# The backward segment of a recurrent-memory attention block: output projection as column passes, and the segment's heads in two halves

## The chip, the cores and the metric

The kernel runs on one core of a Trainium2 chip. The metric is the device time of one execution in microseconds (us). Before the change three timed runs gave 3111.13, 3111.70 and 3111.64 us, median 3111.64. The profile shown here comes from an execution of its own that took 3105.46 us; its span, from the first to the last instruction in the trace, is 3103.7 us.

## The reference

One transformer block, forward and backward, in bfloat16 data with batch 1, 2048 tokens of 448 features, 16 heads of 256 features each, and a gated feed-forward net of 1792. Attention is recurrent: the tokens come in 64 segments of 32, and each segment attends over 8 memory rows and its own 32 rows (40 rows, `L`). The first 8 output rows of a segment are the memory of the next.

```python
for s in range(n_seg):
    h = concatenate([mem, x[:, 32*s : 32*s + 32]], axis=1)        # 8 + 32 rows
    q, k, v = (einsum('btd,dhe->bhte', h, W) for W in (Wq, Wk, Wv))
    scores = where(mask, einsum('bhqe,bhke->bhqk', q, k) * scale, -1e9)
    p = softmax(scores)
    o = einsum('bhte,hed->btd', einsum('bhqk,bhke->bhqe', p, v), Wo)
    mem, out = o[:, :8], o[:, 8:]
# h = x + attention(layernorm(x));  result = h + ffn(layernorm(h))
```

The kernel returns the block's output and the gradients with respect to `x`, `mem0`, the four attention weights and the three feed-forward weights, for a given gradient of the output.

In the backward direction the segments run from 63 down to 0, one after another, since the gradient of a segment's 8 memory rows is what the segment before it starts from. Per segment: the gradient of the output rows goes back through `Wo` (call the result dO, 40 rows of 4096 columns); dP = dO v^T and dv = p^T dO; dS = p * (dP - rowsum(dP * p)); dk and dq from dS and its transpose; and the three of them go back through `Wv`, `Wk`, `Wq` to the 40 input rows, of which the first 8 are the gradient carried to the next segment in the order.

## The kernel before

The program runs through a forward chain, the feed-forward net, the backward chain of 64 segments and a tail for the weight gradients. The change is in `backward_chain`, with one small edit in the feed-forward phase (two pad columns). Four segments make a tile of 128 tokens. `r` counts a tile's segments and goes 3, 2, 1, 0. A chunk is 128 of the 4096 head columns, so there are 32 chunks (`MC`), two per head, and the 448 features lie in 4 chunks (`KC`) of which the last holds 64.

In one segment the engines do this:

- The input is one window of `do_roll`: the transposed gradient of the 32 token rows, loaded for a whole tile by `prep_tile`, and of 8 memory rows which the segment before has written at L1226. That write is the carried gradient.
- Output projection, L1151: 128 matmuls, each with 128x128 of the transposed `Wo` as stationary side and 40 columns of `do_roll` moving. They give dO turned (`doT`), in 4 PSUM banks that DVE and ACT take out in turn. 16 transposes (L1160) make the token-major copy `dO_sb`, which ACT takes out (L1161).
- Gradients of the probabilities, L1169: 32 matmuls of `doT` with `vT` into one bank `pD`. DVE then makes the gradients of the scores in four instructions over all 8 pairs of heads, L1176 to L1181, the last of which writes the block-diagonal `dS_bd`.
- Heads, L1128 (`heads`, `head_mm`): v from `dO_sb` and the probabilities `P_bd`, k from `Q_sb` and `dS_bd`, q from `K_sb` and `dST_bd`; 16 matmuls of 80 columns each, in three banks. Each bank is taken out in two pieces, the 32 token rows into `blk` and the 8 memory rows into `lo`. Evacuations carry L75 on DVE and L76 on ACT, since one helper (`k.evac`) makes them all.
- Turned scores, L1209: 16 small matmuls with the identity turn `dS_bd` into `dST_bd`, by way of bank `pT`, a DVE and an ACT evacuation.
- Rows, L1200 (`rows_in`): 32 matmuls each for v, k and q, which run four at a time in tiles of 32 columns and all accumulate in one bank `pH`. DVE and ACT take it out (L1218, L1219), four matmuls with a selection matrix (L1222) fold the four strips, and L1226 writes the next segment's carried gradient.

Once a tile, at `r == 0`, the memory rows of the tile go through the same weights (L1264, 96 matmuls), and after L1271 and L1279 the layer norm's backward step writes 128 rows of the result (`ln_bwd`, lines L252 to L263 on DVE and ACT). These instructions have no hurry and are spread by the scheduler as fills into the following segments.

The order of instructions on every engine is fixed when the program is built. A scheduler takes the code above as a graph; what stands under `k.prio.crit()` goes first, and `tc.issue_after` ties an instruction to another. Each engine then works through its own list in order and stops where a semaphore is missing. PSUM banks come from small rings (`k.ps1`, `k.fx1`, `k.po1`), so a group of matmuls also waits until its bank's last reader is done.

Loads are issued from two queues. SP loads `vT`, `Q_sb` and `K_sb` (`load_v`, `load_seg`) for the next segment. POOL loads the segment's probabilities (`P_sb`, L1082), spreads them into `P_bd` with two copies (L1084) and issues the stores of finished tiles.

Of the kernel before, what the change touches and what calls it, by code (L numbers as in the profile page):

```python
# [9 lines left out]
FP32 = mybir.dt.float32  # L10
BF16 = mybir.dt.bfloat16
# [225 lines left out]
def cj(j):  # L237
    return (j % 2) * 16 + j // 2
# [574 lines left out]
def ffn_phase(k: _K, back):  # L813
# [32 lines left out]
    for i in range(2):  # L846
        nc.gpsimd.memset(dhb_b[i][:, D:DP], 0.0)
# [88 lines left out]
    for n, gi in enumerate(turns):  # L936
# [67 lines left out]
        for tt in range(G):  # L1004
# [16 lines left out]
            nc.scalar.copy(out=dh_b[:, 0:D], in_=dh_t)  # L1021
            nc.gpsimd.dma_start(out=dr["DHb"][rows, :], in_=dh_b)
# [9 lines left out]
def backward_chain(k: _K):  # L1032
# [9 lines left out]
    WoT_sb = W(0, KC, HD)  # L1042
# [7 lines left out]
    dO_sb = A(52, 16, P)  # L1050
    doT = A(56, 32, 64)
# [5 lines left out]
    P_bd, dS_bd, dST_bd = [B(1.25 * i, 8, 2, L) for i in range(3)]  # L1057
    Pb = [B(3.75 + 0.625 * i, 8, L) for i in range(2)]

    def prep_tile(t):  # L1060
        if t < 0:
            return
        nc.sync.dma_start_transpose(out=dhx, in_=dr["DHb"][t * P:(t + 1) * P, :])
        s0 = (4 * t) % NWIN
        for kc in range(KC):
            nc.gpsimd.tensor_copy(out=do_roll[:, kc, s0:s0 + 4, 0:SEG], in_=dhx[:, kc, :].rearrange("p (g j) -> p g j", g=4))

# [3 lines left out]
    def load_seg(s):  # L1071
# [8 lines left out]
        P_sb = Pb[s % 2]  # L1080
        with tc.issue_after(k.pool_op.ins) if s == NSEG - 1 else nullcontext():
            nc.gpsimd.dma_start(out=P_sb.rearrange("p h n -> p (h n)"), in_=dr["P_all"][s])  # L1082
        for g in range(2):
            pool_op = nc.gpsimd.tensor_copy(out=P_bd[64 * g:64 * g + L, :, g, :], in_=P_sb[64 * g:64 * g + L, :, :])  # L1084
        stores("mid", s, pool_op.ins)
# [6 lines left out]
    def stores(place, seg, ins):  # L1092

        for fn in pending.pop((place, seg), []):
            with tc.issue_after(ins):
                fn()

    for tl in (Q_sb, K_sb, P_bd, dS_bd):
        nc.gpsimd.memset(tl, 0.0)
# [6 lines left out]
    nc.sync.dma_start(out=WoT_sb[:, 0:3, :], in_=dr["To"][:, 0:3, :])  # L1106
    nc.sync.dma_start(out=WoT_sb[0:64, 3, :], in_=dr["To"][0:64, 3, :])
    nc.gpsimd.memset(WoT_sb[64:P, 3, :], 0.0)
# [5 lines left out]
    nc.vector.memset(doT[:, :, L:64], 0.0)  # L1114
    nc.gpsimd.memset(dST_bd, 0.0)
    nc.gpsimd.memset(dxT[:, KC - 1, :], 0.0)
    om = k.f32("f1", DP, "omb")
    nc.gpsimd.memset(om[:], 0.0)

    def c12(ps, b):  # L1120
        n = min(12, 32 - 12 * b)
        return 12 * b, n, ps[:, 0:n * L].rearrange("p (c n) -> p c n", n=L)

    def head_mm(ps, lhs, rhs_bd, turned):
        for cl in range(16):
            b, i = divmod(cl, 6)
            at = 8 * (cl // 4 % 2) + 4 * (cl // 8) + cl % 4 if turned else cl
            nc.tensor.matmul(ps[b][:, i * 2 * L:(i + 1) * 2 * L], lhsT=lhs[:, at, :],  # L1128
                             rhs=rhs_bd[:, cl // 2, :, :].rearrange("p g n -> p (g n)"), start=True, stop=True)

    for s in range(NSEG - 1, -1, -1):
# [7 lines left out]
        if r == 2:  # L1139
            prep_tile(t - 1)  # L1140
        if s < NSEG - 1:
            load_seg(s)

        with k.prio.crit():
            pss = [k.ps1() for _ in range(4)]
            for j in range(MC):
                c = cj(j)
                b, jj = divmod(j, 8)
                for kc in range(KC):
                    with tc.issue_after(k.last_dh.ins) if s == NSEG - 1 and j == 0 and kc == 0 else nullcontext():  # L1150
                        nc.tensor.matmul(pss[b][:, jj * L:(jj + 1) * L], lhsT=WoT_sb[:, kc, c * P:(c + 1) * P],  # L1151
                                         rhs=do_roll[:, kc, sl, :], start=(kc == 0), stop=(kc == KC - 1))
            for b in range(4):
                k.evac(doT[:, 8 * b:8 * b + 8, 0:L], pss[b][:, 0:8 * L].rearrange("p (c n) -> p c n", n=L), "vsvs"[b])

            def token_major(hf):
                ph = k.ps1()[:].bitcast(BF16)
                for i in range(8):
                    c0 = 2 * (8 * hf + i)
                    nc.tensor.transpose(ph[:, i * P:(i + 1) * P], doT[:, c0:c0 + 2, :].rearrange("p c n -> p (c n)"), ident[:, :])  # L1160
                nc.scalar.copy(out=dO_sb[:, 8 * hf:8 * hf + 8, :], in_=ph.rearrange("p (c n) -> p c n", n=P))  # L1161
            token_major(0)
            token_major(1)
            pD = k.ps1()
            for h in range(8):
                for g in range(2):
                    for dc in range(DC):
                        j = 2 * (2 * h + dc) + g
                        nc.tensor.matmul(pD[64 * g:64 * g + 64, h * L:(h + 1) * L], lhsT=doT[:, j, :], rhs=vT[:, 2 * h + dc, L * g:L * g + L],  # L1169
                                         start=(dc == 0), stop=(dc == DC - 1), skip_group_check=True)  # L1170
            if s == 0:
                k.tl.grads(0)
                k.tl.outs(0, 7, 0, 6)
            pD3 = pD[:, 0:8 * L].rearrange("p (h n) -> p h n", n=L)
            prod = k.f32("f2", 8 * L, "prod")[:].rearrange("p (h n) -> p h n", n=L)
            nc.vector.scalar_tensor_tensor(out=prod, in0=pD3, scalar=k.scale, in1=P_sb, op0=ALU.mult, op1=ALU.mult)  # L1176
            rsum = smal.tile([P, 8], FP32, name="rsum")
            nc.vector.tensor_reduce(out=rsum[:], in_=prod, axis=AX.X, op=ALU.add)
            nc.vector.scalar_tensor_tensor(out=prod, in0=pD3, scalar=k.scale, in1=rsum[:].unsqueeze(2).to_broadcast([P, 8, L]),
                                           op0=ALU.mult, op1=ALU.subtract)  # L1180
            nc.vector.tensor_tensor(out=dS_bd, in0=prod.unsqueeze(2).to_broadcast([P, 8, 2, L]), in1=P_bd, op=ALU.mult)  # L1181
# [3 lines left out]
            def heads(nm, lhs, rhs):  # L1185
                pps[nm] = [k.ps1() for _ in range(3)]
                head_mm(pps[nm], lhs, rhs, nm != "v")
                for b in range(3):
                    c0, n, v = c12(pps[nm][b], b)
                    k.evac(blk[nm][:, c0:c0 + n, r * SEG:(r + 1) * SEG], v[:, :, M:L], "vsv"[b])  # L1190
                for b in range(3):
                    c0, n, v = c12(pps[nm][b], b)
                    k.evac(lo[nm][:, c0:c0 + n, r * M:(r + 1) * M], v[:, :, 0:M], "svs"[b])
                if s == 0:
                    k.tl.outs(*{"v": (7, 9), "k": (9, 10), "q": (10, 11)}[nm], 0, 6)

# [6 lines left out]
            heads("v", dO_sb, P_bd)  # L1203
            rows_in("v", WvT_sb, 0, MC)
            heads("k", Q_sb, dS_bd)
            pT = k.ps1()
            for h in range(8):
                for g in range(2):
                    nc.tensor.matmul(pT[64 * g:64 * g + L, h * L:(h + 1) * L], lhsT=dS_bd[:, h, g, :],  # L1209
# [306 lines left out]
```

## Time and profile before

| what | value |
|---|---|
| median of three runs | 3111.64 us |
| span of the profiled execution | 3103.7 us |
| mean TensorE clock granted | 0.988 |
| PE busy, whole span | 2914.8 us (94%) |
| DVE busy | 1331.6 us (43%) |
| ACT busy | 1112.6 us (36%) |
| POOL busy | 674.7 us (22%) |
| first and last carried gradient (L1226) | 1382.88 and 2394.50 us |
| first matmul of the tail that needs the backward chain's stores (L1396) | 2430.74 us |

All busy times are sums over one engine's instructions; engines work side by side, so they don't add up to the span. PE is TensorE's matmuls, PEld its weight loads. DVE is VectorE, ACT ScalarE, POOL GpSimd, and SP only issues transfers. A matmul's own duration contains its way through the array; when many follow each other, it is the distance between starts that costs time. A piece "PE psf L1151 x128" in the chain of waits is a run of 128 matmuls of line 1151, and the number before it is the time that the run holds in the chain. Releasers ("<-") name what ended an engine's idle time.

From the first to the last L1226 are 1011.62 us, with 62 distances between them: 16.32 us a segment on average, so the backward chain is about a third of the program.

### The profile page before, as it was taken

How to read it: one execution, taken by the hardware profiler on the slowest of the kernel's cores; microseconds unless marked ns; L12 is line 12 of the kernel's file. 1: busy time of each engine (PE TensorE's matmuls, PEld its weight loads, DVE VectorE, ACT ScalarE, POOL GpSimd, SP SyncE). 2: the span in 40 equal slices, each digit the busy share in tenths (PEclk: the TensorE clock that was granted, in tenths of full speed). 3: DMA queues.
4: the chain of work that ended last, by engine and by line, in shares of the span. 5: the costliest groups of instructions: out<-in, count | busy, mean ns of one | idle time of the engine just before them, and what ended most of it. 6: DMA issues, size and time to landing. Idle time of an engine off the chain costs nothing.

```text
span 3103.7 us, 108341 instructions
## 1 busy us (share of the span) xinstructions
PE 2914.8 (94%) x47640; PEld 1735.5 (56%) x47650; DVE 1331.6 (43%) x3381; ACT 1112.6 (36%) x2634; POOL 674.7 (22%) x1511
## 2 busy tenths in 40 slices
PE   5899999989988999989999999999999899999998
PEld 3555555545544555666666666666666454444443
DVE  3555455455455576654444444544445101111110
ACT  2444344344444544443434344444344001111110
POOL 2222222222222222321122111221211111212111
PEclk9999999999999999999999999999999899999999
DMA  6567756756756899984455445555544999969951
GB/s 242 136 172 178 183 162 167 191 158 167 189 161 182 276 222 228 221 298 119 133 150 143 128 137 142 143 139 136 141 138 133 284 267 244 190 181 199 192 160 57
DMA packets 739084, 550.12 MB, mean 177 GB/s; under 512 B 600052, under 2 KB 634852, under 8 KB 736180
## 3 DMA queue, kind: packets, MB, share of 16 engines
q1 hardware_dynamic: 687380, 389.19, 51.5%
q0 software_dynamic: 51232, 154.00, 14.9%
q8 instruction: 374, 6.13, 0.8%
q14 instruction: 98, 0.80, 0.1%
HBM read 168.01 MB, written 234.23 MB: 130 GB/s over the span
## 4 chain that ended last, share of the span: by engine, by line
PE 72%; issue 11%; DVE 6%; DMA 5%; ACT 4%; POOL 2%; SPq 1%; ACTq 0%; POOLq 0%; DVEq 0%
PE po L1200 7%; PE psf L1151 7%; PE psf L535 6%; PE psf L652 5%; PE po L697 4%; PE psf L1375 4%; PE psf L890 4%; PE psf L1128 4%; PE psf L1396 4%; PE fx L1264 3%; PE fx L1014 3%; PE fx L464 2%; PE psf L1222 2%; DVE arA L75 2%; PE psf L549 2%
## 5 line engine op out<-in xcount | busy, mean ns | idle before, releaser
L75 DVE CAST arA<-psf 128x256 bf16<-128x256 f32 (+3 forms) x933 | 427.2, 480 | 808.6 <-PE psf L1375 275.2
L76 ACT CAST arA<-psf 128x96 bf16<-128x96 f32 (+5 forms) x915 | 352.4, 409 | 1036.6 <-PE psf L1375 261.2
L1200 PE MATMUL po<-arW,arA 128*32 128x448 bf16 x6144 | 347.3, 355 | 4.6 <-DMA arW<-Tq 3.5
L1375 PE MATMUL psf<-arW,arA 128*128 128x512 bf16 x980 | 247.1, 380 | 0.0
L1375 PEld LDWEIGHTS <-arA 128*128 128x128 bf16 x1440 | 136.0, 98 | 164.8 <-issue 13.8
L1151 PEld LDWEIGHTS <-arW 128*128 128x128 bf16 x8192 | 213.4, 96 | 25.0 <-issue 25.0
L1151 PE MATMUL psf<-arA,arW 128*128 128x40 bf16 x8192 | 217.0, 180 | 6.2 <-DVE arA L1226 5.1
L652 PE MATMUL psf<-arW,arA 128*64 128x512 bf16 x1536 | 219.0, 386 | 0.0
L1200 PEld LDWEIGHTS <-arA 128*32 128x32 bf16 x6144 | 152.0, 96 | 115.8 <-ACT arA L76 9.4
L535 PE MATMUL psf<-arW,arA 128*32 128x512 bf16 x3072 | 193.8, 385 | 12.5 <-DVE arA L738 12.5
L76 ACT CAST arB<-psf 128x64 bf16<-128x64 f32 (+3 forms) x384 | 121.8, 318 | 153.1 <-PE psf L539 109.7
L697 PE MATMUL po<-arW,arA 128*32 128x256 bf16 (+1 forms) x4096 | 144.2, 267 | 10.5 <-DVE arA L75 7.5
L890 PE MATMUL psf<-arW 128*128 128x256 bf16 (+1 forms) x1288 | 146.3, 274 | 1.3 <-DVE arA L956 0.7
L890 PEld LDWEIGHTS <-arW 128*128 128x128 bf16 (+1 forms) x1344 | 102.4, 97 | 51.4 <-issue 40.8
L1161 ACT COPY arA<-psf 128x1024 bf16<-128x1024 bf16 x128 | 123.3, 1015 | 2.2 <-PE psf L1160 0.4
L1128 PEld LDWEIGHTS <-arW 128*128 128x128 bf16 x2048 | 86.4, 99 | 61.8 <-issue 56.9
L535 PEld LDWEIGHTS <-arA 128*32 128x32 bf16 x3072 | 70.6, 97 | 90.0 <-DVE arA L738 18.1
L76 ACT COPY arA<-psf 128x512 bf16<-128x512 bf16 (+3 forms) x142 | 84.3, 594 | 99.9 <-DVE arA L75 90.3
L464 PE MATMUL fx<-arA,arW 128*128 128x64 bf16 (+1 forms) x2048 | 84.3, 196 | 32.4 <-ACT arB L76 19.2
L697 PEld LDWEIGHTS <-arA 128*32 128x32 bf16 x4096 | 95.9, 98 | 32.9 <-DVE arA L75 10.5
L1128 PE MATMUL psf<-arB,arW 128*128 128x80 bf16 x2048 | 96.8, 201 | 13.6 <-DVE arB L1181 5.2
L1436 POOL DMA_DIRECT2D out_dram<-arA x96 | 51.7, 546 | 249.7 <-DVE arA L75 246.9
(290 smaller groups left out, 4645.7 us busy)
## 6 DMA issues: line engine op xcount, KB each, us to landing
arW<-T SPq DMA_DIRECT2D x256, 128.0 KB
X_o<-arA SPq DMA_DIRECT2D x37, 512.0 KB
T<-arA SPq DMA_DIRECT2D x64, 256.0 KB
X_v<-arA POOLq DMA_DIRECT2D x32, 512.0 KB, 4.9
X_k<-arA POOLq DMA_DIRECT2D x32, 512.0 KB, 4.0
X_q<-arA POOLq DMA_DIRECT2D x32, 512.0 KB, 3.1
out_dram<-arA POOLq DMA_DIRECT2D x90, 128.0 KB, 3.5
VG<-arA SPq DMA_DIRECT2D x64, 160.0 KB
```

The costliest lines, as they stand in the source:

```text
L75: return nc.vector.tensor_copy(out=out, in_=in_)
L76: return nc.scalar.copy(out=out, in_=in_)
L464: nc.tensor.matmul(banks[w][:, i * 64:(i + 1) * 64], lhsT=lhsT, rhs=xr[lo:hi, kc, :], start=(kc == 0 and i == 0), stop=(kc == KC - 1), ski ...
L535: nc.tensor.matmul(banks[w][32 * q:32 * q + 32, :], lhsT=hT_roll[:, kc, sl, M:L], rhs=(Wq_sb, Wk_sb)[w][:, kc, col(q, b)], start=(kc == 0) ...
L652: nc.tensor.matmul(pV[b][64 * g:64 * g + 64, 0:512], lhsT=hT_flat[:, kc, sl * L:sl * L + 64], rhs=Wv_sb[:, kc, n * 512:(n + 1) * 512], sta ...
L697: nc.tensor.matmul(pO[32 * q:32 * q + 32, 0:w], lhsT=xblk[:, j, r * SEG:(r + 1) * SEG], rhs=Wo_sb[:, cj(j), 256 * dh:256 * dh + w], start= ...
L890: nc.tensor.matmul(ps[fp][:, f2 * 256:(f2 + 1) * 256], lhsT=Wt[lo:hi, kc, c * P:(c + 1) * P], rhs=xT[lo:hi, kc, :], start=(kc == 0 and f2 ...
L1128: nc.tensor.matmul(ps[b][:, i * 2 * L:(i + 1) * 2 * L], lhsT=lhs[:, at, :], rhs=rhs_bd[:, cl // 2, :, :].rearrange("p g n -> p (g n)"), st ...
L1151: nc.tensor.matmul(pss[b][:, jj * L:(jj + 1) * L], lhsT=WoT_sb[:, kc, c * P:(c + 1) * P], rhs=do_roll[:, kc, sl, :], start=(kc == 0), stop ...
L1200: nc.tensor.matmul(pH[32 * (j % 4):32 * (j % 4) + 32, 0:D], lhsT=blk[nm][:, j, r * SEG:(r + 1) * SEG], rhs=WT[:, cj(j), :], start=(nm == " ...
L1375: nc.tensor.matmul(pa[2 * kc + g][:, 0:w], lhsT=lhs_of(b)[:, kc * P:(kc + 1) * P], rhs=rhs_of(b, g), start=(b == 0), stop=(b == nblk - 1), ...
L1396: k.last_mm = nc.tensor.matmul(pa[i][:, 0:D], lhsT=lhs_of(b, i), rhs=rhs_of(b), start=(bi == 0), stop=(bi == len(nblk) - 1))
```

## The change

The output projection is turned around for 32 of a segment's 40 rows: 24 token rows and the 8 carried ones. `do_roll` becomes the stationary side, in tiles of 32 columns, and the transposed `Wo` moves with 512 columns (`wide_pass`), into two banks; dO then comes out token-major, and 8 transposes of 128x128 in two halves (`half_turned`) give `doT`. The other 8 token rows ("rest" rows, which are known ahead) are done for four segments together, once a tile (`rest_pass`, `wide_turned`), and POOL copies one segment's share into `doT`.

The v heads become `values`: 16 matmuls with token-major dO as stationary side and 160 columns of probabilities, in two parts (rest rows with `Pq_rest`, the others with `Pq_b`) that accumulate in three banks. All six pieces are taken out by ACT. The probabilities are loaded in the layout that these matmuls need by small DMAs from POOL's queue (4 a segment in `load_p`, 16 a tile in `load_p_rest`), and `rest_probs` on DVE masks the shared rest rows for one segment. `P_bd` is gone.

Gradients of probabilities, gradients of scores, k and q heads and turned scores each run in two halves of the heads, interleaved. Score gradients take five instructions per half. A half of k or q heads has a bank of its own and shares a third one.

Further: the pad columns of the feed-forward phase's `dhb_b` are filled by a copy in place of a memset; L1222's fourth matmul becomes two of 64 columns; `do_roll` is prepared one segment earlier in the tile.

```diff
@@ backward_chain, loads
+    def load_p(s):
...
+        for q in range(4):
+            g, x = divmod(q, 2)
+            src = dr["P_all"][s, 64 * g + M:64 * g + L].rearrange("i (b x h n) -> i b x h n", b=2, x=2, n=L)
+            nc.gpsimd.dma_start(out=Pq_b[s % 2][32 * q:32 * q + 32].rearrange("p (b h) q n -> p b h q n", b=2)[:, :, :, 2 * x + g, :],
+                                in_=src[:, :, x])
@@ backward_chain, helpers
+    def wide_pass(banks, out, lhs_of, after=None):
...
+        for b in range(2):
+            for kc in range(KC - 1):
+                for q in range(4):
+                    with tc.issue_after(first.ins):
+                        nc.tensor.matmul(banks[b][32 * q:32 * q + 32, :], lhsT=lhs_of(kc, 0, P), rhs=WoT_sb[:, kc, col(q, b)],
+                                         start=False, stop=(kc == KC - 2), skip_group_check=True)
+        for b in range(2):
+            k.evac(out[:, b, :], banks[b][:], "vs"[b])
+
+    def half_turned(pt, src, dst, b):
+        for i in range(4):
+            nc.tensor.transpose(pt[:, (4 * b + i) * P:(4 * b + i + 1) * P], src[:, b, i * P:(i + 1) * P], ident[:, :])
+        k.evac(dst[:, 16 * b:16 * b + 16], pt[:, 512 * b:512 * b + 512].rearrange("p (c n) -> p c n", n=32), "vs"[b])
+
+    def rest_probs(s):
+        nc.vector.tensor_tensor(out=Pq_rest, in0=Pr_b[(s // 4) % 2].unsqueeze(2).to_broadcast([P, 4, 4, L]),
+                                in1=gmask[:, s % 4, :].unsqueeze(1).unsqueeze(3).to_broadcast([P, 4, 4, L]), op=ALU.mult)
@@ backward_chain, one segment
-            pss = [k.ps1() for _ in range(4)]
-            for j in range(MC):
...
-                        nc.tensor.matmul(pss[b][:, jj * L:(jj + 1) * L], lhsT=WoT_sb[:, kc, c * P:(c + 1) * P],
-                                         rhs=do_roll[:, kc, sl, :], start=(kc == 0), stop=(kc == KC - 1))
...
-            token_major(0)
-            token_major(1)
+            wide_pass([k.ps1(), k.ps1()], dO_sb, lambda kc, lo, hi: do_roll[lo:hi, kc, sl, M:L])
...
+            pt = k.ps1()[:].bitcast(BF16)
+            half_turned(pt, dO_sb, doT[:, :, M:L], 0)
+            pv += [k.ps1() for _ in range(3)]
+            values(1)
+            half_turned(pt, dO_sb, doT[:, :, M:L], 1)
...
+            def grad_of_probs(b):
+                for h in range(4 * b, 4 * b + 4):
...
+                            nc.tensor.matmul(pD[64 * g:64 * g + 64, h * L:(h + 1) * L], lhsT=doT_flat[:, j * L:j * L + 64],
+                                             rhs=vT[:, 2 * h + dc, L * g:L * g + L],
...
+            grad_of_probs(0)
+            grad_of_scores(0)
+            values(0)
+            grad_of_probs(1)
+            grad_of_scores(1)
+            for b in (0, 2, 1):
+                of, v = v_out(b)
+                k.evac(of(blk["v"])[:, :, :, r * SEG:(r + 1) * SEG], v[:, :, :, M:L], "s")
+                k.evac(of(lo["v"])[:, :, :, r * M:(r + 1) * M], v[:, :, :, 0:M], "s")
...
-            heads("v", dO_sb, P_bd)
-            rows_in("v", WvT_sb, 0, MC)
-            heads("k", Q_sb, dS_bd)
...
-            rows_in("k", WkT_sb, 0, 20)
-            heads("q", K_sb, dST_bd)
-            rows_in("k", WkT_sb, 20, MC)
+            rows_in("v", WvT_sb, 0, 12)
+            heads("k", Q_sb, dS_bd, 0)
+            turned_scores(0)
+            rows_in("v", WvT_sb, 12, MC)
+            if r == 0 and t > 0:
+                rest_pass()
+            heads("k", Q_sb, dS_bd, 1)
+            turned_scores(1)
+            heads("q", K_sb, dST_bd, 0)
+            rows_in("k", WkT_sb, 0, 12)
+            heads("q", K_sb, dST_bd, 1)
+            rows_in("k", WkT_sb, 12, MC)
+            if r == 0 and t > 0:
+                wide_turned(dO_rest, R)
+            if s > 0:
+                rest_probs(s - 1)
             rows_in("q", WqT_sb, 0, MC)
```

## The prediction

> **What bounds the kernel now.** I read the page's slices first (PE at 9 in nearly all of them, the granted clock at full speed), then the table of windows for the stretch in which whole backward segments run, then the chain of waits of one segment, then the waits and the costliest groups of that stretch. The windows' columns are stretch, length, and busy time of PE, PEld, DVE, ACT and POOL.
>
> ```profile
> 1420.00:1900.00 480.00, 462.21 (x10907) 329.50 (x10905) 229.24 (x582) 198.89 (x516) 98.22 (x227) 1.00 0.52 140
> ```
>
> PE is busy 96% of it, DVE 48%, ACT 41%, POOL 20%, and the DMA engines 52%. Nothing but PE's stream of instructions can be the bound, and little of it is idle. One segment's chain says how that stream runs (start, length, what):
>
> ```profile
> 1905.41 3.30 PE psf L1151 x128
> 1908.71 0.97 PE psf L1160 x16
> 1909.68 0.62 PE psf L1169 x32
> ...
> 1910.32 0.46 PE psf L1128 x8
> 1910.78 0.49 PE fx L1264 x8
> 1911.27 0.42 PE psf L1128 x8
> 1911.69 1.63 PE po L1200 x32
> ...
> 1914.04 1.05 DVE arA L75 x3
> 1915.10 0.40 DVE arB L75
> ...
> 1915.57 0.43 ACT arB L76
> ...
> 1916.04 0.73 PE psf L1128 x16
> 1916.78 2.19 PE po L1200 x43
> ```
>
> From one carried gradient (L1226) to the next are 16.03 us here. PE goes through output projection (3.30), transposes (0.97), gradients of probabilities (0.62), v heads (0.46 + 0.42), v rows, k heads, and stands in the chain almost throughout. The one real stop is 1914.04 to 1916.00: the turned scores pass DVE and ACT before the q heads start. The fills L1264 and the rows L1200 (both matmuls of 448 columns, 0.051 each) cover what they can.
>
> ```profile
> L1181 DVE TENSOR_TENSOR arB<-prod,arB 128x640 bf16<-128x640 f32 x30 | 24.7, 825 | 0.0
> L1161 ACT COPY arA<-psf 128x1024 bf16<-128x1024 bf16 x60 | 57.8, 1015 | 0.7
> L75 DVE CAST arA<-psf 128x384 bf16<-128x384 f32 x89 | 49.5, 556 | 48.1 <-PE psf L1128 48.1
> L1176 DVE SCALAR_TENSOR_TENSOR prod<-psf,arB 128x320 f32<-128x320 f32 x30 | 14.8, 492 | 53.2 <-PE psf L1169 53.2
> L1082 POOL DMA_DIRECT2D arB<-P_all x30 | 16.3, 543 | 113.4 <-DVE prod L1176 105.7 <-DVE arB L1181 7.7
> ```
>
> The last four engine rows give the prices below; their idle shares say that DVE and ACT wait for PE, not PE for them. The starts of L1226 lie 17.04, 15.83, 16.05 and 16.04 us apart, 64.96 a tile.
>
> **What the skill says.** "TensorEngine Tiling (Array Packing)", Performance Considerations, proposes for a moving side of at most 32 columns to swap the operands and run four column tiles. The trace agrees: the forward chain's L535 is such a pass (24 matmuls of 512 columns, 379 ns each, overlapping), and with L539's 8 it takes 1.75 us (803.56 to 805.31), against 3.30 for L1151. The same page, Key Properties, says that a change of tile mode drains the array; the trace shows no price for it apart: bounds 0 and 0.1 us a switch, and I take 0.05. Its PSUM Bottleneck says that after such a speed-up the evacuations may bind. "PSUM — Partial Sum Buffer", PSUM bank collisions raise a hardware error, asks to guard PSUM by bank and quadrant; that is why pieces that share a bank wait for each other's reader here. No run shows a collision.
>
> **PE's work, part by part.** Removed per segment: L1151 3.30, L1160 0.97, v heads 0.88, together 5.15. Added: the wide pass 1.75; 8 transposes at 0.97/16, 0.49; values, 16 matmuls of 160 columns, for which the nearest row is the q heads' 0.73/16 = 0.046 for 80 columns: between 0.046 and 0.1, I take 0.075, so 1.20; once a tile the rest pass and its transposes, (1.75 + 0.49)/4 = 0.56. Together 4.00, and some 4 more mode switches, 0.2. The stream is shorter by 0.95 us a segment. Gradients of probabilities, k and q heads, turned scores and rows keep their counts. L1340's two half matmuls instead of one: 0.
>
> **What stands in order on it.** Followed along the order in which the changed program issues its instructions, with the durations of the rows (an evacuation of 128x512 f32 on DVE 0.556 + 128 x 1.07 ns = 0.69, the slope from the 256 and 384 rows; half of L1176, 0.49 - 160 x 1.04 = 0.33). A segment whose carried gradient is ready at 0, r = 2:
> - wide pass to 1.9; DVE's evacuation of bank 0 1.5 to 2.2. Half-turn 0 on PE 2.4 to 2.8, its evacuation on DVE to 3.3; half-turn 1 writes the same bank and waits for it: 3.35 to 3.75. The values with the rest rows fill the gap.
> - half-turn 1's evacuation on ACT to 4.4. The first half's last gradient matmul takes 64 columns of doT from a 40-column chunk and so reads the next chunk, which ACT writes: the first half isn't free before the second. It ends at 4.9 (before: 4.9, since 3.30 + 0.97 + 0.62 = 4.89). So nothing is gained yet.
> - score gradients, half 0 on DVE: 4 steps of 0.33 and two of 0.25 to 0.31, 5.0 to 6.6; half 1 must first get pD from PE, which DVE's L1179 of half 0 holds up, then 6.6 to 8.8 with a k evacuation (0.55) and a dST evacuation (0.3) in between. Both halves are 3.2 us of DVE against 2.28 before.
> - v rows run in this time and wait for ACT's six v_out evacuations (0.48 + 0.24 + 0.38 + 0.21 + 0.48 + 0.24 = 2.03). k half 0 at 6.8, turned scores 7.1, v rows to 8.8; k half 1 and turned half 1 follow dS half 1 at 9.0, q half 0 at 9.6, q half 1 at 10.9 (it waits for ACT's last dST piece), then some 45 rows to 13.8, and the 1.6 to 2.5 us of sum, L1222 and L1226 as before: 15.4.
> So r = 2 takes 15.4 against 15.83 to 16.05, and r = 3 by the same steps 15.1: of the old stop of 1.96 us a gain of 0.4 to 0.9 is left. The two others give it back:
> - r = 1: v_out and values wait for ACT, which has the tile's copies ahead of them; G of half 0 is 0.65 later (5.6), the halves end at 9.3; 17.2 against 16.04.
> - r = 0: the layer norm's L254 (0.62), L257, L259, L260 (0.68) and L263 (2 x 0.42) stand on DVE ahead of the half-turn's evacuation and of half 0; half 0 starts at 6.4. The rest pass fills PE while half 1 is on DVE, but its transposes are added: 18.6 against 17.04.
> Sum by tile: 15.1 + 15.5 + 17.2 + 18.6 = 66.4 (r = 2 unrounded 15.46). The same walk of the order before gives 66.1 where the trace has 64.96, so its error is 2% and only the difference counts: 0.3 more. Two entries were taken high: DVE can begin bank 0 before bank 1's last matmuls, 0.13 a segment or 0.5 a tile, and the values at 0.046 would save another 0.5. That is a gain of 0.2 to 0.7 a tile; I take 0.45; times 15.75 tiles 7 us.
>
> **Other edits.** P_bd's two POOL copies (0.45 each) go; POOL gets a copy (0.5) and 4 DMA issues a segment and 16 a tile, (4 + 4) x 0.545 = 4.4 us. POOL was busy 98.2/480, or 3.3 us of a segment, so 7.3 of 16: hidden, as the pieces are issued one segment or a tile ahead. Stores queued behind them on POOL have a segment of slack. Their 512 + 64 small packets a segment, at 0.31 x 480 x 16/59888 = 0.04 us a packet on the hardware queue, are 23 us over 16 engines, 9 points more than 52%: hidden. SP gets no new DMA inside a segment. DVE's rest_probs (about 0.83, L1181's shape) replaces nothing and lies between half-turn 0 and half 0; in the chain above it ends at 4.4, before DVE is needed. FFN: a pad copy on ACT of 64 columns, 0.2 x 16, ACT isn't the bound there: 0, at most 3. Start: rest pass, transposes and copies before the first segment, 6 to 7 us of latency, in place of a 6.8 us stall (DVE waits for a store there before the first L1226 at 1382.88): -4 to +3, I take 0. End: the tail's first matmul waits 13.02 us for X_o loads whatever PE does: -1 to 0.
>
> Profiled span 3103.7, run of it 3105.46; the three timed runs are 6 us longer (3111.64), and the difference is set against these: 3111.64 - 7 = 3104.6, say 3104.
>
> **Rivals.**
> (a) The waits are hidden by fills, rows and rest pass, as the old stop largely was; then the shorter stream counts: 0.95 x 63 = 60, 3052. For it: PE at 96% today, with DVE and ACT at less than half. Against: the half chain holds eight handovers in a row where there were four. With half of it realised 3080.
> (b) DVE's queue becomes the bound in the segment's middle. The mechanism: two half chains of score gradients (3.2 us) with other evacuations between them, behind in-order layer norm and rest_probs. It decides when half 0 begins later than about 5.3 us after the carried gradient, averaged over the four segments (I have 5.0, 5.0, 5.6, 6.4, mean 5.5, with stages behind it shorter by 0.3). Each 0.3 later is 0.3 x 63 = 19: 3130; 0.5, from mode switches at 0.1 too, 3143.
> (c) POOL's or the queue's many small loads come late and the values wait: 16 issues, 8.7 us, in one segment. 2 us a tile would be 32: 3144. Against: a tile of lead.
> (d) Halving does nothing since half 0 waits for half 1's evacuation; then only the shorter stream and the longer DVE chain remain: 0.95 less 0.92, no change, 3110.
>
> **How the numbers follow.** Forecast with (d) beside it, within 20 us of 3107: 0.45, of which three fifths lie under 3105.4. (a), whole or half: 0.22. (b) 0.27 and (c) 0.06. A measurement of this kernel tells 0.2%, 6.2 us, from no change. Faster by more than that: 0.22 + 0.25 = 0.47; within: 0.17; slower: 0.33 and a little of the forecast, 0.36. The range takes half of (a) and its margin, 3062, to (b)'s far end, 3142. Cases of both signs hold most of the chance; the forecast's own range is 3088 to 3120.
>
> **What would show it.** Right: the wide pass about 1.8 us; the chain through L1176's successor twice a segment; half 0 starting near 5.0 in two segments of a tile and later in the two others; starts of the carried gradient unequal, 15 to 15.5 twice and 17 or more twice. Wrong: equal segments of 15.3 (a), PE below 90% with DVE in most of the chain (b), or DMA from P_all as a releaser (c).

## The result, and the profile after

The changed kernel is slower: median 3163.25 us (four runs, 3157.21 to 3172.47) against 3111.39 (the three runs of above and one more), a ratio of 1.0173 (95% interval 1.0146 to 1.0200). Its profiled execution has a span of 3159.7 us, 56.0 more than the one before.

Three marks in the two traces say where. The first carried gradient is written at 1396.47 us instead of 1382.88 (13.6 later). From the first to the last are 1051.4 us instead of 1011.6 (39.8 more). What follows takes 711.9 instead of 709.2 (2.7 more).

The 13.6 is too small a figure for the start, since executions differ in how far the earlier phases have got. A mark that lies ahead of the changed part, the start of DVE's last step of 3584 columns in the feed-forward phase, shows it (first two lines before, last two after):

```profile
1335.27 2.02 DVE L977 TENSOR_TENSOR arA<-arA 128x3584 bf16<-128x3584 bf16 x1
1382.88 0.19 DVE L1226 CAST arA<-psf 128x32 bf16<-128x32 f32 x1 [2.01 <-PE psf L1222]
1328.55 2.02 DVE L975 TENSOR_TENSOR arA<-arA 128x3584 bf16<-128x3584 bf16 x1
1396.47 0.19 DVE L1344 CAST arA<-psf 128x32 bf16<-128x32 f32 x1 [3.46 <-PE psf L1340]
```

From the mark to the first carried gradient are 47.6 us before and 67.9 after: the start costs 20.3 us, and this execution happened to be 6.7 us ahead at the mark (in e3, e7 and e10 below the mark lies at 1334.8 to 1335.5). So the loss lies at the start and in the steady part of the backward chain, nearly two thirds of it in the second. There a tile takes 68.17 us instead of 64.95, and its four segments (named by the one that runs after the carried gradient) change like this:

| r | before | after |
|---|---|---|
| 2 | 16.04 | 15.73 |
| 1 | 17.04 | 18.07 |
| 0 | 15.83 | 19.2 (18.4 in the first two full tiles) |
| 3 | 16.05 | 15.15 |

The window of the steady part, same columns as in the prediction:

```profile
1420.00:1900.00 480.00, 474.17 (x7911) 268.71 (x7907) 251.70 (x657) 180.48 (x619) 211.98 (x424) 0.99 0.57 135
```

PE is busy 98.8% of it, after 96.3%, with 7911 matmuls instead of 10907. It hardly waits at all; it does fewer matmuls in more time. A stretch of the chain of waits of the changed kernel, from the middle of an r = 0 segment, shows how:

```profile
1908.32 0.48 PE po L1303 x5
1908.80 0.14 PE psf L1248
1908.94 0.29 PE po L1303
1909.23 0.33 PE fx L1118 x4
1909.56 0.87 PE po L1303 x15
1910.42 0.36 PE psf L1248 x16
1910.79 0.30 PE po L1303 x3
1911.09 0.39 PE psf L1286 x8
```

L1303 are the rows (L1200 before), L1248 gradients of probabilities, L1286 heads, L1118 the wide pass's first step. One row matmul alone holds PE for 0.29 us, three for 0.30, five for 0.48, fifteen for 0.87. In the chain before, 32 took 1.63 and 43 took 2.19. All these, before and after, fit 0.10 + 0.19 for each started group of four: the rows run four at a time in 32-column tiles, so by these figures a group that isn't full costs as much as a full one, and each run pays 0.10 once, which is put down to the change to another kind of matmul (e1 and e2 test it). In one tile's chain the rows and the memory rows' matmuls stand in some 25 pieces before and 49 after.

The clock is the second thing. Windows of the changed kernel around the start of that segment (the figure before the last two is the granted clock):

```profile
1895.46:1898.87 3.41, 3.27 (x64) 1.88 (x62) 1.11 (x2) 1.78 (x7) 1.94 (x4) 1.00 0.78 206
1898.87:1902.28 3.41, 3.41 (x32) 2.30 (x24) 0.50 (x2) 0.56 (x3) 3.41 (x7) 1.00 0.26 51
1902.28:1905.69 3.41, 3.41 (x34) 1.41 (x35) 1.08 (x4) 1.06 (x5) 3.01 (x7) 0.50 0.06 5
```

From the third full tile on it falls to half for 3.41 us once a tile. The kernel before has no such fall between 1420 and 2410 us.

### The profile page after: what moved, and what is told of

It reads as the page before. It is cut to its first block, busy times and chain, and to the rows that moved or that the text cites. A ratio compares the mean times of both kernels' runs of the same rounds, so it can differ in the third digit from the quotient of the medians.

```text
span 3159.7 us, 97558 instructions
## 1 busy us (share of the span) xinstructions
PE 2985.3 (94%) x41762; PEld 1622.1 (51%) x41762; DVE 1405.9 (44%) x3608; ACT 1095.4 (35%) x2938; POOL 934.6 (30%) x1972
## 4 chain that ended last, share of the span: by engine, by line
PE 75%; issue 10%; DMA 6%; DVE 4%; ACT 3%; POOL 2%; SPq 1%; POOLq 0%; ACTq 0%; DVEq 0%
PE po L1303 10%; PE psf L535 5%; PE psf L652 5%; PE psf L1493 4%; PE po L697 4%; PE psf L1514 4%; PE fx L1382 3%; PE psf L1124 3%; PE psf L1286 3%; PE psf L888 3%; PE psf L1223 2%; PE fx L1012 2%; PE fx L464 2%; PE psf L549 2%; PE psf L1337 2%
## 5 line engine op out<-in xcount | busy, mean ns | idle before, releaser
L76 ACT CAST arA<-psf 128x512 bf16<-128x512 f32 (+2 forms) x1107 | 385.7, 396 | 984.9 <-PE psf L1493 261.2
L75 DVE CAST arA<-psf 128x384 bf16<-128x384 f32 (+3 forms) x613 | 344.9, 573 | 707.3 <-PE psf L1493 275.2
L1303 PE MATMUL po<-arW,arA 128*32 128x448 bf16 x6144 | 415.8, 356 | 4.2 <-ACT arA L76 4.2
L1493 PEld LDWEIGHTS <-arA 128*128 128x128 bf16 x1440 | 136.3, 98 | 165.8 <-issue 15.6
L1303 PEld LDWEIGHTS <-arA 128*32 128x32 bf16 x6144 | 152.2, 95 | 120.1 <-ACT arA L76 19.7
L76 ACT CAST arB<-psf 128x64 bf16<-128x64 f32 (+3 forms) x512 | 146.1, 288 | 185.6 <-PE psf L539 108.1
L76 ACT COPY arA<-psf 128x512 bf16<-128x512 bf16 (+3 forms) x206 | 122.0, 593 | 140.1 <-DVE arA L75 90.1
L1108 POOL DMA_DIRECT2D arW<-P_all x256 | 144.4, 570 | 33.3 <-DMA arW<-P_all 19.2
L1286 PE MATMUL psf<-arB,arW 128*128 128x80 bf16 x2048 | 121.6, 202 | 4.3 <-DVE prod L1256 0.3
L1382 PE MATMUL fx<-arW,arA 128*32 128x448 bf16 x1024 | 124.1, 357 | 0.0
L1286 PEld LDWEIGHTS <-arW 128*128 128x128 bf16 x2048 | 89.5, 99 | 66.8 <-issue 51.4
L75 DVE COPY arA<-psf 128x512 bf16<-128x512 bf16 (+2 forms) x204 | 87.1, 427 | 80.1 <-PE psf L549 52.8
L535 PEld LDWEIGHTS <-arA 128*32 128x32 bf16 x3072 | 70.1, 96 | 89.0 <-DVE arA L738 18.1
```

The costliest lines, as they stand in the source:

```text
L75: return nc.vector.tensor_copy(out=out, in_=in_)
L76: return nc.scalar.copy(out=out, in_=in_)
L535: nc.tensor.matmul(banks[w][32 * q:32 * q + 32, :], lhsT=hT_roll[:, kc, sl, M:L], rhs=(Wq_sb, Wk_sb)[w][:, kc, col(q, b)], start=(kc == 0) ...
L1108: nc.gpsimd.dma_start(out=Pr_b[t % 2][32 * q + M * i:32 * q + M * i + M].rearrange("p (b h) n -> p b (h n)", b=2), in_=src[:, :, x])
L1286: nc.tensor.matmul(ps[bank][:, i * 2 * L:(i + 1) * 2 * L], lhsT=lhs[:, at, :], rhs=rhs[:, cl // 2, :, :].rearrange("p g n -> p (g n)"), st ...
L1303: nc.tensor.matmul(pH[32 * (j % 4):32 * (j % 4) + 32, 0:D], lhsT=blk[nm][:, j, r * SEG:(r + 1) * SEG], rhs=WT[:, cj(j), :], start=(nm == " ...
```

## The experiments

All are compared with the kernel before on the same chip. "Tile" is the steady time of four segments in the profiled execution; "changes" are the changes between 32-column matmuls of the wide kind and all others that a tile's built PE order holds, counted from the order alone. The first carried gradient moves by up to 19 us between executions with the same start (the changed kernel and e5), since earlier phases differ; the time since the mark, in brackets, is 67.8 to 68.9 in the changed kernel, e3, e5, e7 and e11, whose starts are the same.

| run | ratio (95% interval) | first carried (since the mark) | tile | changes |
|---|---|---|---|---|
| before | 1 | 1382.9 (47.6) | 64.95 | 45 |
| after | 1.0173 (1.0146 to 1.0200) | 1396.5 (67.9) | 68.17 | 82 |
| e1 spares between | 1.0325 (1.0286 to 1.0364) | 1384.4 (49.0) | 71.67 | 101 |
| e2 spares in a block | 1.0053 (1.0027 to 1.0079) | 1385.1 (48.2) | 66.55 | 53 |
| e3 fours | 1.0019 (1.0008 to 1.0029) | 1403.7 (68.9) | 64.94 | 74 |
| e4 first loads on SP | 1.0202 (1.0177 to 1.0227) | 1410.5 (73.3) | 68.17 | 82 |
| e5 fold steps apart | 1.0306 (1.0273 to 1.0339) | 1415.6 (68.1) | 70.7 to 72.5 | 63 |
| e6 first loads after stores | 1.0178 (1.0145 to 1.0211) | 1420.0 (73.6) | 68.17 | 82 |
| e7 two banks | 1.0165 (1.0133 to 1.0197) | 1403.6 (68.1) | 67.6 to 69.2 | 69 |
| e8 fours, fold apart, after stores | 1.0143 (1.0105 to 1.0181) | 1406.7 (70.9) | 68.3 | 59 |
| e9 fours, early loads | 0.9988 (0.9975 to 1.0002) | 1402.2 (58.8) | 64.93 | 74 |
| e10 no rest pass | 1.0001 (0.9981 to 1.0021) | 1400.2 (65.4) | 64.67 | 75 |
| e11 fours, whole heads | 1.0040 (1.0022 to 1.0057) | 1399.6 (67.8) | 65.53 | 69 |
| e12 fours, early loads, two banks | 1.0098 (1.0070 to 1.0126) | 1397.6 (59.7) | 65.9 to 71.3 | 63 |
| e13 fours, loads third | 1.0017 (1.0000 to 1.0034) | 1396.9 (64.3) | 64.94 | 74 |
| e14 eights, loads third | 1.0019 (1.0003 to 1.0034) | 1398.6 (65.7) | 65.1 to 66.1 | 68 |
| e15 eights, rest banks | 1.0029 (1.0017 to 1.0041) | 1399.0 (63.5) | 65.2 to 66.7 | 52 |
| e16 fours, fold apart, rest banks | 0.9993 (0.9979 to 1.0008) | 1404.6 (63.3) | 63.75 or 65.2 | 60 |
| e17 rest pass tied | 1.0123 (1.0095 to 1.0152) | 1401.5 (64.9) | 67.03 | 79 |
| e18 (the kernel of e16) | one run, 3105.24 us | 1398.2 (63.0) | 63.75 or 65.2 | 60 |

**What a break costs (e1, e2).** Both edit the kernel before, with spare matmuls that are in nobody's way:

```diff
-            rows_in("q", WqT_sb, 0, MC)
+            for j in range(0, MC, 4):
+                with tc.issue_after(last.ins):
+                    rows_in("q", WqT_sb, j, j + 4)
+                last = spare(k.row, 1) if j < MC - 4 else None
```

In e2 it is `with tc.issue_after(spare(k.row, 7).ins): rows_in("q", WqT_sb, 0, MC)` instead.

> The kernel before, with 7 spare matmuls (128x128 stationary, 40 columns, written to an unused part of the bank of the last step, read by nobody) put one after each four of a segment's 32 q rows. Theory F (fragments): in both traces a run of n row matmuls in 32-column tiles holds PE for 0.10 + 0.19 us per started four, so breaking one run of 32 into eight adds 7 x 0.10 and the spares 7 x 0.026: 0.88 us a segment, 55 us in all, about 3167. Theory W (waits of the half chains cost the time, fragments are only their trace): only the spares' own time counts, 7 x 0.026 = 0.18 a segment, 12 us, about 3123.

> The control: the same 7 spare matmuls, all in one block ahead of the 32 q rows of a segment. F: one more break (0.10) and the spares (0.18): 0.28 us a segment, 18 us, about 3129. W: 12 us, about 3123. The difference to the run with the spares in between is 37 us by F and none by W.

The chain of e1, then of e2 (L1222 is here the spare's line):

```profile
1918.75 0.12 PE psf L1222
1918.87 0.30 PE po L1200 x4
1919.17 0.12 PE psf L1222
1919.30 0.30 PE po L1200 x4
```

```profile
1915.53 0.28 PE psf L1222 x7
1915.81 1.63 PE po L1200 x32
```

The same instructions in another order cost 71.67 - 66.55 = 5.12 us a tile, for 48 more changes: 0.107 us a change between these rows (32-column tiles) and a matmul on the whole array. It is paid in both directions (the spare takes 0.12 where its share in the block is 0.04, the four rows 0.30 instead of 0.19), so a break costs twice what I expected, and e1 lost 101 us instead of 55. The waits' theory, 12 us for both, falls.

**Fours held together in the changed kernel (e3).**

```diff
+                    with k.prio.crit() if j % 4 else nullcontext(), tc.issue_after(k.quad.ins) if j % 4 else nullcontext():
-                    nc.tensor.matmul(pH[32 * (j % 4):32 * (j % 4) + 32, 0:D], ...
+                        mm = nc.tensor.matmul(pH[32 * (j % 4):32 * (j % 4) + 32, 0:D], ...
+                    if j % 4 == 0:
+                        k.quad = mm
```

> The changed kernel, where of each four row matmuls (token rows and memory rows alike) the second to fourth are queued right behind the first, so that a run holds whole fours. The instructions are the same. In the built order the runs of row matmuls go from 669 to 591 and the price 0.10 + 0.19 per started four from 470 to 427 us in all. F: 43 us less in the chain, about 3121 against 3163. W: rows fill the waits less finely, so no gain: 3163 or slower. Start unchanged: first carried gradient near 1396.

The same is done for the memory rows. The median is 3116.9, 46 us less than the changed kernel with the same instructions. A tile is back at 64.94, of which 0.8 us is the clock, which no longer falls. From the price, 8 changes and 2.2 us of unfilled fours come to 3.1 us; measured without the clock 2.4. Other instructions move with the fours (the tile's f32 folds now lie spread among other work), so the 2.4 needn't be the fours' alone.

**The waits (e7, e11, e12, e14, e15).** In e7 and e12 each half of the gradients of probabilities gets its own bank; e11 is e3 with the order of the heads taken from the kernel before; e14 and e15 hold eight rows together (`j % 8`), e15 with `wide_pass([k.ps1(), k.ps1()], ...)` in the rest pass.

> The changed kernel with a PSUM bank of its own for each half of the gradients of probabilities, so that PE's second half no longer waits for DVE's first half (in the second to last segment of a tile PE stands 1.04 us for it). W: that wait goes in the one segment in which it is visible, 1 us a tile, 16 us, and DVE's second half starts earlier elsewhere: 3130 to 3147. F: in the built order 69 changes of mode a tile instead of 82, 0.2 us more for unfilled fours: 1.2 us a tile, 19 us, with the wait 2.2 us, 35 us: about 3128. If one more bank out of five makes other groups wait for their banks: 3163 or slower.

> Fours held together, and the order of the kernel before for the heads: k heads whole, turned scores whole, 20 k rows, q heads whole (score gradients stay in halves). Against the run with fours alone (3117). F: 69 changes a tile instead of 74, 0.6 us, 9 us less: 3108. W: the old stop of 2 us a segment before the q heads comes back in so far as rows don't cover it, 0.5 to 1 us a segment: 3148 to 3180. This is what the halves of heads and turned scores are worth by themselves.

> As the run with fours and early loads, with a PSUM bank for each half of the gradients of probabilities. F: 63 changes of mode a tile instead of 74 and 0.2 us of unfilled fours: 1.35 us a tile, 21 us, and the wait in one segment 0.6 us a tile, 9 us: about 3067 to 3076 if the early loads work. As in the changed kernel with two banks, where one segment gained 0.57 us and the next lost 0.8: no gain, 3097.

> As the run before, with runs of eight row matmuls held together instead of four. F: 68 changes of mode a tile instead of 74 and 0.2 us more unfilled: 0.45 us a tile, 7 us less than that run. W (fills too coarse for the waits): no less, or more by up to 0.5 us a segment.

> As the run with eights, and the rest pass takes its two PSUM banks from the ring of five instead of the two banks that the memory rows' steps use, so that it stands in one piece where it is traced. F: 52 changes of mode a tile instead of 68, unfilled 0.2 instead of 0.4 us: 1.9 us a tile, 30 us less than the run with eights, faster than the kernel before by 25 to 45 us. If the ring of five is then short and groups wait for banks: as the run with eights or slower.

```diff
-            pD = k.ps1()
+            pDs = [k.ps1(), k.ps1()]
```

None gained. In e7 the r = 1 segment fell by 0.57 and r = 0 rose by 0.8; in e12 r = 0 took 17.8 to 23.2, since PE then waited for the loads of K (in all 12.9 us of its waits between 1420 and 2400 us end with a load from T0k). e11, where the fours stay and only the halves of k, q and turned scores are undone, loses 0.6 us a tile (r = 3 goes from 15.2 to 16.2, r = 1 from 17.7 to 17.3): that is all the halves of the heads are worth. e15 has the fewest changes, and by the price alone should have been fastest. PE's own waits show what took the gain. Between 1420 and 2400 us it stood 42.5 us in e15 and 17.0 in e3, 1.7 us a tile more, and the largest entry in e15 (us in all, times, longest) is nearly absent in e3, which stands second:

```profile
PE psf L1133 <- DVE arA L75: 16.2, 25, 1.2
PE psf L1131 <- DVE arA L75: 0.3, 2, 0.2
```

These are transposes that wait for DVE's evacuation. The 22 changes fewer than in e3 are worth 2.4 us a tile by the price; 1.7 of that went to waits, and the rest isn't placed. So the waits are real, and the fragments are what they are paid with: fine filling costs changes of mode, and coarse filling leaves waits open. Fours are about the best point found, and there a tile costs what it cost before.

**Once a tile (e5, e8, e10, e16).** e10 leaves the rest pass out of all tiles but the first; e5, e8 and e16 place the fold steps (pl, pX and the layer norm) three segments later in the program, behind the next tile's segment r = 1, with the f32 folds queued behind that segment's values.

```diff
-            om2 = k.f32("f3", D, "om2")
+            def finish(t=t, px=px, after=None):
+                om2 = k.f32("f3", D, "om2")
...
+                    with tc.issue_after(after.ins) if after is not None else nullcontext():
+                        nc.tensor.matmul(pl[0:m, kc * 32:(kc + 1) * 32], lhsT=om2[:, kc * P:kc * P + m], rhs=sel[:],
...
+        if r == 1 and t < NT - 1:
+            k.finish(after=k.mark)
```

> The changed kernel without the rest pass and its 8 transposes in all tiles but the first (the rest rows of the first tile are used throughout, so the results of the other tiles are not the reference's); all else as it is. Rest pass and transposes are 1.75 + 0.70 us of PE a tile, and with them go 6.6 changes of mode (0.7): if PE is simply full, 3.15 us a tile, and 0.85 more if the clock then stays up: 47 to 60 us, 3103 to 3116. If the rest pass lies in time that PE would otherwise stand, it gives less than half of that: 3140 or more.

> The changed kernel, where the f32 matmuls that fold and turn a tile's memory rows (the pl and pX steps, 12 of them, once a tile) are queued behind the values of the second segment of the next tile, so that they no longer stand in one stretch with the carried gradient's f32 matmuls. Theory T (clock): in the changed kernel the granted clock falls to 0.5 for 3.4 us once a tile, at the end of a stretch of 3.9 us with next to nothing but small f32 matmuls; without that stretch no clock below 1.0 from 1420 us on, and 0.85 us a tile back, 11 us. Theory F (by now 0.107 us for each change between 32-column and other matmuls, from the two runs with spares, and 0.19 per started four): the new order has 63 changes a tile instead of 82 and 0.4 us less for unfilled fours: 2.4 us a tile, 38 us. Both: about 3114. T alone 3152. Neither (the waits W): 3163.

> Fours held together, fold steps apart and the first loads behind the stores, all in the changed kernel. F with T: 59 changes of mode a tile instead of 82 (2.4 us), unfilled fours from 2.4 to 0.2 us, the clock 0.85: 5.5 us a tile, 63 us a segment set, 85 us, and the start 10 to 17: about 3065, faster than the kernel before (3112). W: fills come less finely into the waits, so no better than the run with fours alone less the start: 3105.

> Fours held together, first loads in the third place on SP, fold steps behind the second segment's values as in the run that lost by it, and the rest pass on the ring of five banks. In the earlier run with fours and fold steps apart three segments of a tile took 15.0 us and the fourth 21 to 22, since the rest pass waited there for a bank that the layer norm held, up to the segment's end. If that bank was the whole loss, the fourth segment takes 15 + 1.75 + 0.70 + 1.7 = 19 at most and a tile 64: 15 us less than with fours and third-place loads (3115), about 3100. With the layer norm's own instructions ahead of the tail as there, 66 and 3130.

e10 gains 3.5 us a tile and 47 us in all, near what was expected of a full PE (4.0 with the clock); the rest pass, with the clock that falls beside it, is as dear as the whole loss. e5 and e8 missed by far: segments r = 2 and r = 1 came down to 15.0 to 15.6, r = 0 rose to 20 to 25, and the clock kept falling. The edit didn't do what e5's expectation wanted: there the folds start at 1735.96 us, 14.5 us into a segment r = 0, and the carried gradient's f32 matmuls follow at 1744.49 with only the layer norm and the rest pass between, so that the two still share a stretch. e5 is therefore no test of the clock's cause. The chain of e8 at the end of such a segment (DVE's layer norm, then the rest pass):

```profile
1514.66 0.69 DVE t L260
1515.35 0.04 issue
1515.39 0.62 PE fx L1118 x3
1516.01 2.68 PE fx L1124 x24
1518.69 0.37 PE psf L1131 x4
1519.06 0.64 PE psf L1344 x6
```

The rest pass needs a bank that the layer norm still reads, and PE takes its orders in turn, so all of it, at half clock (2.68 instead of 1.41), stands in front of L1344, here the fold of the carried gradient. In e16, with other banks for the rest pass, r = 0 takes 17.7 or 19.1 and a tile 63.75 or 65.2: 0.9993, as fast as the kernel before in spite of a start that takes 16 us longer since the mark. So the bank was the larger part of the loss in e8, together with the longer falls of the clock beside it (6.8 us in most tiles of e8, 3.4 in e16).

**The clock (e16 again).**

> A second look at the kernel with fours, fold steps apart and rest pass on banks of its own, for the clock: in its first profile 10 of 15 fourth segments took 19.1 to 19.4 us, with the granted clock at 0.5 for 3.41 us, and 5 took 17.7 without. The starts of these stretches lay whole multiples of 3.413 us apart. If the clock is set in windows of a free-running grid, another execution has the same two lengths, 17.7 and 19.1, in another pattern, and again whole multiples. If it is fixed by the program, the same tiles fall.

Both executions had the two lengths, 17.7 and 19.1 us, but not in the same tiles: 11 falls in each between 1420 and 2425 us, each 3.41 us long, with starts 19 or 38 times 3.413 us apart. In the changed kernel they lie 20 times 3.413 = 68.27 apart, and the tile takes 68.17; in e5 a fall lasts 6.83 or 10.24 us, two or three times as long. So which tile has a fall isn't laid down by the program, and the starts fit a fixed grid of 3.413 us. That a fall comes when a stretch with little work in the array covers one window of the grid fits all this but isn't shown. Nor is it shown that these stretches are those of the small f32 matmuls (L1389, L1337, L1397, with the four quick L1118), though the place suggests it, and in e3, where they lie spread among other work (between 1874 and 1884 us in one tile), no fall came after 1420 us; no run changed these alone. The length agrees with the Trainium skill, "TensorE: Matmul & The Clock Gate", Part 1, which gives a free-running window of 3413 ns. The price here is 1.4 us a fall in e16, by which its 11 falls cost some 15 us (an estimate), and 0.8 in the changed kernel, some 10 us for its 12 falls up to 2425 us.

**The start (e4, e6, e9, e13, e17).** e4 takes SP for the first loads, e9 and e13 also move them up, e6 queues them on POOL behind the last store of DHb, e17 ties the rest pass.

```diff
 # e4, e9, e13
+        eng = nc.sync if s == NSEG - 1 else nc.gpsimd
 # e6
+    with tc.issue_after(k.last_dhb.ins):
+        load_p(NSEG - 1)
+        load_p_rest(NT - 1)
 # e17
-                rest_pass()
+                rest_pass(k.mark)
```

> The changed kernel with the loads of the first segment's and first tile's probabilities (P_all: 1 + 4 + 16 transfers) issued from SP's queue in place of POOL's; all later ones stay. If the late start (first carried gradient 1396.5 against 1382.9) is POOL's queue, in which the feed-forward phase's stores DH and DHb stand behind these loads, it comes back by 10 to 13 us: about 3151, first carried gradient 1383 to 1386. If the start is late because of the rest pass and its copies, nothing: 3163.

> The changed kernel with the first tile's loads of P_all queued on POOL behind the feed-forward phase's last store of DHb, instead of among and ahead of the last stores. If these stores were what the start waited for, the first wide pass comes back from 1393 to about 1360 and the first carried gradient from 1396.5 to about 1386 (it then waits for 21 issues of 0.57 us = 12 us and 3 us of landing): 10 us, about 3153. If the start isn't POOL's order: 3163.

> Fours held together, and the first segment's and first tile's loads of P_all issued from SP right behind the loads of Wo, some 25 us earlier than in the run that moved them to SP, at a time when SP's queue is idle and before the 8 MB of the other weights. If the late start is these loads' landing (and on POOL the stores behind them), the first carried gradient comes to about 1383 as before, against 1404 with fours alone: 20 us, about 3097, faster than the kernel before. If they land late wherever they are issued: 3117.

> As fours with early loads, but the first loads of P_all stand on SP between the loads of Wk and of Wq instead of ahead of Wv, Wk and Wq, whose late landing the early loads had brought (the first q rows waited 24 us for Wq). If the start is only a matter of what stands in SP's queue, Wq is issued near 1376 and the first carried gradient comes to about 1388 against 1402: 14 us, about 3097. If the DMA engines' load at that time is what counts (72 to 84% busy), whatever the order: 1400, 3111.

> The changed kernel with the rest pass of each tile queued behind the values of the fourth segment, in which it is traced. In the changed kernel's first tile PE has the next rest pass three segments early, in front of the first fold of the carried gradient, and there it waits until the next tile's load of DHb has landed (20 us after its issue). If that is what makes the start late, the first carried gradient comes 3 to 8 us earlier (1389 to 1393, its next limit being the rows that wait for ACT until 1390.5); the built order has 78.6 changes of mode a tile instead of 82, 0.35 us: together 9 to 13 us, about 3152. If the start is POOL's queue alone: 1396 and 3158.

The first segment's wide pass in fact ran near 1365 in the changed kernel too; the one at 1393 that e6's expectation names is the next tile's rest pass, which PE has in its order among the first folds. By the time in the span all five missed on the first carried gradient (e13's second case, 1400, came nearest), but the mark tells more. Behind it e17, which moves that rest pass, gained 3.0 us, the low end of its 3 to 8 (e10, which has no such pass, 2.5), and e9 10 us against e3, half of what was expected. e13 came out 5.5 us later than e9 instead of 14 earlier, and e4 and e6 lost 5 to 6. In the changed kernel the chain goes through POOL's loads (L1108), a feed-forward store behind them, and a load of DHb:

```profile
1355.60 0.36 POOL arW L1108
...
1357.16 14.23 DMA Zt<-arW
...
1371.95 20.02 DMA arA<-DHb
```

Ahead of these lines the loads hold up the feed-forward phase too, since DVE has `rest_probs` in its order in front of that phase's last steps:

```profile
1348.55 0.83 DVE L1143 TENSOR_TENSOR arB<-arW,arA 128x640 bf16<-128x640 bf16 x1 [11.83 <-DMA arW<-P_all]
```

DVE stood 11.83 us for the load, and PE 7.26 us for DVE. In e4 and e9 PE has no such stop. With the loads on SP (e4) the values waited for them until 1396; issued earlier (e9) they landed in time, but Wq, behind them in SP's queue, took the 24.36 us that this line of e9's chain shows:

```profile
1372.53 24.36 DMA arW<-Tq
```

Behind Wk (e13) DHb's load was last again. The 21 small loads take 0.57 us each to issue on POOL and 0.64 on SP, 12 to 13 us in all, and the longest landing in the chain is 15.0 us in the changed kernel, 18.1 in e13 and 26.9 in e4; in each of these runs something that the first segment needs was behind them. What a start without them would give wasn't tried. e17's gain of 13 us lies for the most part in the tiles (67.03; the clock fell twice in place of 12 times).

## Why the prediction was wrong

**PE's work, part by part** failed, in one term: "some 4 more mode switches, 0.2" a segment. There are 9 more a segment, and one costs 0.107, not the 0.05 I took (just above my upper bound of 0.1): 1.0 us a segment. Unfilled fours, which the sum didn't have at all, add 1.3 us a tile. That is 5.3 us a tile in place of 0.8, and the 3.8 us that I had PE save are gone. By pieces this makes PE's stream 0.7 us a tile longer. PE's busy time (98.8% of 68.17 against 96.3% of 64.95) says 4.8, of which 0.8 is the clock; where the other 3.3 come from stays open. The other durations held: wide pass 0.34 + 1.41 = 1.75, values 4.94/64 = 0.077, a DVE step of a half 0.33. Four transposes took 0.33 to 0.37 instead of 0.25 where they follow 32-column matmuls, and 0.22 to 0.35 where they follow values.

**What stands in order on it.** The segments forecast as 15.1, 15.46, 17.2 and 18.6 measured 15.15, 15.73, 18.07 and 18.4 without the clock's fall, and half 0 began 4.6, 4.8, 5.8 and 6.8 us after the carried gradient (5.0, 5.0, 5.6 and 6.4 forecast; the 6.8 holds a fall of the clock). So the walk came near; the order of PE was known. What I did with it failed: I took its error to be the same for both kernels, so that "only the difference counts". It erred in opposite directions, 66.4 against a measured 67.35 and 66.1 against 64.95, and where I had 0.3 us a tile more, 2.4 came without the clock. I then took off 0.75 for entries taken high. The plain comparison of 66.4 with the measured 64.95 gives 1.45 us a tile slower, 23 us. I also gave the 17.04 to r = 0; it belongs to r = 1, so that r = 0, with rest pass and layer norm, is where the loss is.

**Start**: -4 to +3 was forecast; 13.6 came by the time in the span, 20.3 since the mark. POOL's loads were counted as hidden "as the pieces are issued one segment or a tile ahead", which is true of every tile but the first.

**The rivals.** The right side was (b), slower, but not its mechanism: DVE's queue isn't the bound, PE is, at 98.8%. (a) fails, as its shorter stream doesn't exist in this order; (c) holds at the start only. (d)'s wait is there (one of half 0's 16 matmuls comes after the others, the L1248 at 1908.80 above), without deciding.

The fall of the clock stood in no part of the prediction: some 10 us.

## What to carry to other kernels

Count the changes between kinds of matmul in the order that the scheduler makes, not only the matmuls: a change that removes a quarter of the matmuls and splits the rest finer can lengthen a full PE. Fill waits in pieces that fill the tiles of the array (here whole fours), and compare a walk of a new order with measured times, not with another walk. Give the start of a chain its own sum, since what is loaded a tile ahead everywhere else has no tile ahead of it there. Work that is done once a tile needs banks that nothing slow holds.

## What the runs showed of the hardware that was not expected

A change between matmuls in 32-column tiles (448 columns moving) and matmuls on the whole array cost 0.107 us, in each direction (e1 against e2). A run of rows that doesn't fill its last group of four cost as much as if it did: 0.29 us for one row, 0.30 for four. The granted clock fell to 0.5 for 3.41 us on a grid of 3.413 us, also where the profile has PE busy without a gap (3.41 of 3.41 us in the window before the fall), so in these runs busy time alone didn't keep it up.
